# Block 0 of a WKV + FFN + routed-expert kernel: each step of a weight slice's conversion issued half a slice earlier

## The chip, the cores and the metric

The kernel runs on one core of one Trainium2 chip. The metric is device time in microseconds (us) of one execution, smaller is better. Engines are named as in the profile: PE is TensorE's matmul stream (PEld its weight loads), DVE is VectorE, ACT is ScalarE, POOL is GpSimd, SP is SyncE, which issues nearly all transfers.

## What is computed

Three layers, one after the other. The tokens are 4 sequences of 768, the model width is 8 heads of 48 (384).

```python
# 1: linear attention with a per-channel decay
for t in range(S):
    y[:, :, t] = r_t @ (state + (u * k_t) v_t^T)
    state = w * state + k_t v_t^T
# 2: gated feed-forward, d_ff = 1536
g = x @ w_gate
x = (g * sigmoid(g)) * (x @ w_val) @ w_out
# 3: one of 8 experts per token
e = argmax(x @ moe2_w_gate)
out = scale(x, e) * (relu(x @ w1[e]) @ w2[e])
```

## The kernel before

The 3072 tokens are 24 tiles of 128; three tiles form a block, so there are 8 blocks. While the feed-forward layer of block b runs, the attention of the three tiles of block b+1 is woven into it. The feed-forward width of 1536 is cut into 12 weight slices (f = 0 to 11). At the end come the experts.

**The order.** Nothing is scheduled automatically: the order in which the Python code calls the units is the order in which instructions stand in every engine's queue. `b_block` loops over the 12 slices. In iteration f it issues: the gate matmuls g(f) (`b_up`, L491), then the units in `slots[2f]`, then the down projection of slice f-2 (`b_down`, L510), then the value matmuls v(f) (L491 again), then `b_act`, then the units in `slots[2f+1]`. So a slot is half a slice, and whether a unit sits in the even or the odd slot decides whether it stands ahead of or behind `b_act` of that slice. `b_act` is four instructions: the silu on ACT (L499), **the silu product** s = silu(g) * v on DVE (L500), its rounded high part h on ACT (L502), and the remainder on POOL in block 0 (L503). In block 0 g and v use two PSUM banks in turn: g(f+1) waits for the silu of f, v(f+1) for the product of f.

**The conversion, in block 0 alone.** The weights arrive as 64-bit words. Each slice goes through these steps, in order:

- `next_w(f)` (L203): the transfer of 1152 KB by SP. From slice 4 on the data land in one of two buffers, so it waits for the conversion of slice f-2.
- `conv_low(f)` (L214): one ACT instruction takes the lowest bits out of one byte per word.
- `conv_a(f)`: six DVE instructions, three pairs of L229 (shift and or, both inputs in SBUF, result in PSUM) and L230, which make 32-bit floats, the tile `cv`.
- `conv_b(f)`: ACT rounds `cv` to the high part of W (L246), POOL subtracts for the low part (L247).
- `gate_a(f)`: three PE transposes of `cv` into PSUM bank 7 (L255) and their copy by ACT, `gt` (L257).
- `gate_b(f)`: a small product with the router's weights G (L263, bank 7 again), two small copies on ACT (L266 to `wg`, L267), one small subtraction on POOL (L268).

**Attention of a tile in block 0** (`a_place`, over 7 slots from slot 8t): scaling of krT on DVE (L332), a reduction on DVE (L350) and the diagonal matrices from it (L357, eight ACT instructions, for tiles 4 and 5; L359 on POOL for tile 3), scores into banks 6 and 7 (L379), masks on DVE (L384), output and state products (L394, L403, L440; the state product goes to bank 7), output copies (L423, L424), and the state update on DVE that reads bank 7 (`a_state_up`, L454 or L456).

Bank 7 is thus shared by the gate transposes, the gate product, half of the scores and the state product: whoever writes it next waits until the one before has been read by ACT or DVE.

Of the kernel before, what the change touches and what calls it, by code (L numbers as in the profile page):

```python
# [33 lines left out]
BT = 3  # L34
# [18 lines left out]
def kernel(  # L53
# [156 lines left out]
    def conv_low(f):  # L210
        b3 = raws[f].bitcast(U8).rearrange("p (n e) -> p n e", e=8)[:, :, 3]
        t = spare[f] if f in spare else wpool.tile([P, 2 * FG], F32, tag=f"W{f}", name=f"low{f}")
        lows[f] = t[:, 0:FW].bitcast(I32)
        act.activation(out=lows[f], in_=b3, func=AF.Identity, bias=nb, scale=1.0 / 32)  # L214

    def conv_steps(f):
        raw = raws.pop(f)
        r32 = raw.rearrange("p (n two) -> p n two", two=2)
        hi = r32[:, :, 1]
        if f % 2 == 0:  # L220
            t = cpool.tile([P, FW], I32, tag="rows", name="cv", bufs=1)
        else:
            t = apool.tile([P, FW], I32, tag="cv", name="cv", bufs=1)
        cvs[f] = t.bitcast(F32)
        n = lows.pop(f)
        p = bank[5][:, 0:DM].bitcast(I32)

        def word(o):
            dve.scalar_tensor_tensor(p, hi[:, o], 3, n[:, o], ALU.logical_shift_left, ALU.bitwise_or)  # L229
            dve.scalar_tensor_tensor(t[:, o], hi[:, o], 0x3FFFFFFF, p, ALU.bitwise_or, ALU.bitwise_and)  # L230

        return [lambda c=c: word(slice(c * DM, (c + 1) * DM)) for c in range(3)]

    def conv_a(f):
        for u in conv_steps(f):
            u()
# [3 lines left out]
    def conv_b(f, parts=(ALL,)):  # L240
        x = cvs[f]
        if f not in W:
            W[f] = wpool.tile([P, 2, FG], F32R, tag=f"W{f}", name=f"W{f}")
        for o in parts:
            hi, lo = W[f][:, 0, o], W[f][:, 1, o]
            act.copy(out=hi, in_=x[:, o])  # L246
            pool.tensor_tensor(out=lo, in0=x[:, o], in1=hi.bitcast(F32), op=ALU.subtract)  # L247
# [3 lines left out]
    def gate_a(f):  # L251
        x = cvs[f]
        for c in range(KC):
            o = (2 * KC + c) * P
            pe.transpose(bank[7][:, c * P : (c + 1) * P], x[:, o : o + P], ident)  # L255
        gts[f] = t = apool.tile([P, DM], F32, tag="gt", name="gt", bufs=1)
        act.copy(out=t, in_=bank[7][:, 0:DM])  # L257

    def gate_b(f):
        t = gts.pop(f)  # L260
        wg = bank[7][:, DM : DM + 16]
        for c in range(KC):
            pe.matmul(wg, t[:, c * P : (c + 1) * P], G[:, c, :], start=(c == 0), stop=(c == KC - 1))  # L263
        hi, lo = W[f][:, 0, FW:], W[f][:, 1, FW:]
        x = apool.tile([P, 16], F32, tag="wg", name="wg", bufs=2)
        act.copy(out=x, in_=wg)  # L266
        act.copy(out=hi, in_=x)  # L267
        pool.tensor_tensor(out=lo, in0=x, in1=hi.bitcast(F32), op=ALU.subtract)  # L268
# [176 lines left out]
    def a_state_up(i, b):  # L445
        c = i // NB
        if c == TPB - 1:
            return
        m4 = bank[b][:, 0 : 4 * HD].rearrange("s (p e) -> s p e", p=4)
        for j in range(2):  # L450
            q = slice(64 * j, 64 * j + HD)
            sv, m = Sst[i % NB][q, :, j, 0:HD], m4[q]
            if c == 0:
                dve.tensor_copy(out=sv, in_=m)  # L454
            else:
                dve.tensor_tensor(out=sv, in0=m, in1=sv, op=ALU.add)  # L456
# [6 lines left out]
    def a_out(i):  # L463
        a_out_mm(i)
        a_state_mm(i, 7)
        a_decay(i)
        a_out_ev(i)
# [142 lines left out]
    def a_place(slots, i, first):  # L610
        def load():
            if i + 1 < NT:
                a_load(i + 1)

        def load_kr():
            if i + 1 < NT:
                a_load_kr(i + 1)

        def bonus():
            if i + 1 < NT:  # L620
                a_bonus(i + 1)

        def diag():
            a_diag(i, BT < i < 2 * BT)

        def scores():
            a_scores(i)
            a_mask(i)

        slots[first].append(load)  # L630
        slots[first + (i == BT)].append(lambda: a_scale(i))
        slots[first + 1].append(diag)
        e = 1 if i % BT == BT - 1 else 0
        slots[first + 3 - e] += [lambda: a_keys(i), scores]
        slots[first + 5 - e] += [lambda: a_out(i), load_kr, bonus]
        slots[first + 6].append(lambda: a_state_up(i, 7))

    raws = {}

    def next_w(f):  # L640
        if f in (2, 3):
            raws[f] = load_w(f, spare[7 - f][:, 0 : 2 * FW].bitcast(I32))
        elif f < NF:
            raws[f] = load_w(f)
# [157 lines left out]
    with tc.manual_schedule():  # L802
# [59 lines left out]
        for blk in range(NBLK):  # L862
            slots = [[] for _ in range(2 * NF)]

            def clear(first, slot):
                slots[slot].append(lambda: [clear_slots(zts[0], i) for i in (first, first + 1)])

            if blk + 1 < NBLK:
                for t in range(BT):
                    a_place(slots, (blk + 1) * BT + t, 8 * t)  # L870
            if blk == 0:
                slots[0][0:0] = [lambda: conv_low(2), lambda: gate_b(0), lambda: conv_b(1, (GV, OUT)), lambda: gate_a(1), lambda: conv_a(2), lambda: a_state(0, 0)]
                slots[1][0:0] = [lambda: gate_b(1), lambda: conv_b(2), lambda: a_state(1, 1)]
                slots[2][0:0] = [lambda: gate_a(2), lambda: a_state(2, 2), lambda: gate_b(2)]
                for f in range(3, NF):
                    slots[2 * f - 6].append(lambda f=f: conv_low(f))
                    slots[2 * f - 5] += [lambda f=f: conv_a(f), lambda f=f: next_w(f + 2) if f > 3 else None]
                    slots[2 * f - 3].insert(0, lambda f=f: conv_b(f)); slots[2 * f - 3 + (f == 3)].insert(0, lambda f=f: gate_a(f))
                    slots[2 * f - 2].insert(0, lambda f=f: gate_b(f)) if f > 3 else slots[4].append(lambda: gate_b(3))
                slots[19].append(lambda: zts.append(late_consts()))  # L880
            else:
                for o, u in zip((4, 7, 7) if blk == NBLK - 1 else (12, 15, 15), c_units(blk - 1)):
                    slots[o].append(u)
                if blk == 1:
                    for i in range(16):
                        clear(2 * i, 2 + (2 * i) // 3)
                if 2 <= blk < 6:
                    for n in range(3):
                        for k, u in enumerate(scan_units(3 * (blk - 2) + n)):
                            slots[7 * n + 1 + 4 * k].append(u)  # L890
            if blk == NBLK - 1:
                right.close()
                rpool = right.enter_context(tc.tile_pool(name="rpool", bufs=1, side="right"))
                raws12 = [rpool.tile([P, NEF, 2 * DM], F32, name="raw12_0")]
                wfs = [rpool.tile([P, 2, 2 * DM], F32R, name=f"wf{i}") for i in range(4)]
                early = bpool.tile([P, 2, KC, BN], F32R, tag="xT", name="early", bufs=2).rearrange("s h c t -> s (h c t)")
                ge = (EARLY + P - 1) // P
                xd_e = [early[:, i * KC * EARLY : (i + 1) * KC * EARLY].rearrange("s (c t) -> s c t", c=KC) for i in range(2)]
                xs_e = cpool.tile([P, ge, RW - DM], F32, tag="xs_e", name="xs_e", bufs=1)
                xr_e = []  # L900

                def early_gather():
                    xr_e.append(cpool.tile([P, BT, DM + 16], F32, tag="rows", name="xr_e", bufs=1))
                    d_gather(xr_e[0][:, :, 0:RW], 0, EARLY)

                def early_turn(g):
                    d_turn(0, xr_e[0], xd_e, g, EARLY, 7)
                    n = min(P, EARLY - g * P)
                    pool.tensor_copy(out=xs_e[0:n, g], in_=xr_e[0][0:n, g, DM:RW])

                d_load(0)
                slots[12].append(early_gather)
                for f in range(4):
                    slots[11 + 3 * f].append(lambda f=f: d_split(f))
                for g in range(ge):
                    slots[18 + 2 * g].append(lambda g=g: early_turn(g))
            b_block(blk, slots)
# [252 lines left out]
```

## Time and profile before

| what | value |
|---|---|
| median of 3 runs | 871.21 us (870.07 to 871.34) |
| the profiled execution's own time | 870.54 us |
| its span in the trace | 868.7 us |
| PE busy | 823.9 us, 95% of the span |
| DVE, ACT, POOL busy | 55%, 33%, 32% |
| PE's share of the chain that ended last | 89% |

The profile cuts the span into 40 slices of some 21.7 us. PE's busy share is 3 tenths in the first of them, 7 or 8 tenths from the second to the sixth, and 9 tenths or more in all but two behind. Block 0 lies from 34 us (its first gate matmul) to about 139 us. The other numbers of the profile are read in the rows below. Row times are us from the start of the span, durations us, and means of one instruction ns.

### The profile page before, as it was taken

Reading aid. Unit: us, or ns where it says so; the run is one execution under the profiler, and the core shown is the slowest. Engines: PE = TensorE matmul, PEld = TensorE weight load, DVE = VectorE, ACT = ScalarE, POOL = GpSimd, SP = SyncE. Lnnn points to the kernel's source line nnn. Section 1 sums busy time; section 2 is a strip of 40 time slices with the busy share of each in tenths; the row PEclk is TensorE's granted clock in tenths of the full one; section 3 lists DMA queues with packets and bytes.
Section 4 is the critical chain, followed back from the end, with each engine's and each line's share of the span. In section 5 each row is a group of like instructions: output and inputs, shape, how many; then the busy total and the mean of one; then the engine's idle time right before and its main releaser. Section 6 shows DMA issues by size and latency. Waiting matters only on the chain.

```text
span 868.7 us, 13843 instructions
## 1 busy us (share of the span) xinstructions
PE 823.9 (95%) x5427; PEld 794.6 (91%) x5427; DVE 474.7 (55%) x923; ACT 287.2 (33%) x604; POOL 276.7 (32%) x241
## 2 busy tenths in 40 slices
PE   3878889999999999999999999999979999999996
PEld 2668789999999999999999999999979999999996
DVE  8698663354475465566565544333644655555541
ACT  2636452212212221222221222223434444444432
POOL 6766654232344335335244112010100220121022
PEclk9989999999999999999999999999989999999999
DMA  8615415833234222422323211410574443445200
GB/s 259 242 49 207 132 78 153 227 99 114 101 106 136 102 101 80 152 71 82 125 91 116 60 46 47 160 50 1 189 287 143 130 163 122 163 139 167 84 25 35
DMA packets 29768, 104.89 MB, mean 121 GB/s; under 512 B 5175, under 2 KB 14193, under 8 KB 26624
## 3 DMA queue, kind: packets, MB, share of 16 engines
q1 hardware_dynamic: 26368, 94.37, 33.6%
q0 software_dynamic: 3328, 9.56, 2.9%
q8 instruction: 45, 0.74, 0.4%
q14 instruction: 27, 0.22, 0.1%
HBM read 85.84 MB, written 16.41 MB: 118 GB/s over the span
## 4 chain that ended last, share of the span: by engine, by line
PE 89%; DVE 4%; ACT 3%; issue 2%; DMA 2%; SPq 0%; POOLq 0%; DVEq 0%; ACTq 0%
PE bank L491 34%; PE bank L510 18%; PE bank L707 12%; PE bank L724 12%; PE bank L379 3%; PE bank L403 3%; PE bank L394 2%; DVE bank L229 2%; DMA spare<-in_rkv_dram 2%; PE bank L672 1%; PE bank L738 1%; DVE cv L230 1%; PE bank L440 1%; ACT at L357 1%; ACT W L246 1%
## 5 line engine op out<-in xcount | busy, mean ns | idle before, releaser
L491 PE MATMUL bank<-xT,W 128*128 128x384 f32 x1728 | 332.7, 342 | 5.0 <-ACT s L499 4.7
L491 PEld LDWEIGHTS bank<-xT,W 128*128 128x128 f32 x1728 | 305.7, 190 | 8.5 <-ACT s L499 5.1
L510 PE MATMUL bank<-W,h 128*128 128x400 f32 x864 | 175.6, 348 | 0.0
L510 PEld LDWEIGHTS bank<-W,h 128*128 128x128 f32 x864 | 155.9, 189 | 1.7 <-issue 0.4
L502 ACT CAST h<-s 128x384 fp32r<-128x384 f32 x96 | 49.2, 513 | 309.2 <-DVE s L500 309.2
L500 DVE TENSOR_TENSOR s<-s,bank 128x384 f32<-128x384 f32 x96 | 53.0, 552 | 164.4 <-PE bank L491 138.3
L724 PE MATMUL bank<-hd,wf 128*128 128x416 f32 (+1 forms) x576 | 113.7, 343 | 0.0
L724 PEld LDWEIGHTS bank<-hd,wf 128*128 128x128 f32 x576 | 104.2, 188 | 0.6
L746 POOL DMA_INDIRECT out_dram<-yo,ix x32 | 34.4, 1074 | 207.6 <-DVE yo L742 181.6
L503 DVE TENSOR_TENSOR h<-s,h 128x384 fp32r<-128x384 f32 x84 | 60.6, 721 | 48.6 <-ACT h L502 48.6
L711 DVE SCALAR_TENSOR_TENSOR hd<-bank,hd 128x416 fp32r<-128x416 f32 (+1 forms) x64 | 36.6, 573 | 83.8 <-ACT hd L710 83.7
L359 POOL TENSOR_TENSOR at<-ident,a 128x1024 f32<-128x1024 f32 x19 | 36.4, 1914 | 136.4 <-DVE a L350 136.4
L572 POOL DMA_INDIRECT xs<-rows,slot x24 | 25.2, 1050 | 127.4 <-DVE slot L570 88.6
L656 DVE TENSOR_TENSOR wf<-raw,wf 128x768 fp32r<-128x768 f32 x64 | 61.1, 955 | 7.1 <-ACT wf L655 1.5
L707 PE MATMUL bank<-xd1h,wf 128*128 128x416 f32 x192 | 59.8, 370 | 4.6 <-issue 4.6
L499 ACT ACTIVATE s<-bank 128x384 f32<-128x384 f32 x96 | 47.1, 491 | 48.8 <-PE bank L491 48.8
L710 ACT ACTIVATE hd<-bank 128x416 fp32r<-128x416 f32 (+1 forms) x64 | 32.3, 504 | 88.8 <-PE bank L707 87.5
L655 ACT CAST wf<-raw 128x768 fp32r<-128x768 f32 x64 | 52.9, 826 | 0.0
L707 PE MATMUL bank<-xd0h,wf 128*128 128x416 f32 x144 | 43.7, 361 | 0.0
L707 PEld LDWEIGHTS bank<-xd1h,wf 128*128 128x128 f32 x192 | 37.6, 196 | 5.2 <-issue 4.8
L384 DVE COPY_PREDICATED at<-mask,bank 128x512 f32<-128x512 int32 x42 | 28.4, 727 | 16.5 <-POOL at L359 14.5
L461 POOL TENSOR_TENSOR S<-S,pw 128x512 f32<-128x512 f32 x16 | 18.0, 1127 | 58.2 <-PE bank L394 58.2
(181 smaller groups left out, 979.4 us busy)
## 6 DMA issues: line engine op xcount, KB each, us to landing
raw<-in_w_dram SPq DMA_DIRECT2D x36, 768.0 KB, 4.4
raw<-in_w_dram SPq DMA_DIRECT2D x22, 1152.0 KB, 6.9
rkv<-in_rkv_dram SPq DMA_DIRECT2D x21, 576.0 KB, 5.8
krT<-in_krT_dram SPq DMA_DIRECT2D x42, 192.0 KB, 3.4
xs<-zt SPq DMA_DIRECT2D x32, 197.0 KB, 6.4
xr<-xs SPq DMA_DIRECT2D x6, 591.0 KB, 5.7
spare<-in_w_dram SPq DMA_DIRECT2D x2, 1152.0 KB, 9.2
xT<-stage SPq DMA_DIRECT2D x42, 48.0 KB, 2.2
```

What stands on the lines that cost most here:

```text
L359: pool.tensor_tensor(out=af, in0=bc(ident, 1, [P, NH, P]), in1=bc(a, 2, [P, NH, P]), op=ALU.mult)
L491: pe.matmul(ps[i], W[f][:, wl, o : o + P], x[:, xl, c, :], start=(c == 0 and n == 0), stop=(c == KC - 1 and n == 2),)
L499: act.activation(out=s, in_=g, func=AF.Silu)
L500: dve.tensor_tensor(out=s, in0=s, in1=v, op=ALU.mult)
L502: act.copy(out=h[:, 0], in_=s)
L503: (pool if blk == 0 else dve).tensor_tensor(out=h[:, 1], in0=s, in1=h[:, 0].bitcast(F32), op=ALU.subtract)
L510: pe.matmul(bank[t][:, 0 : DM + 16], h[:, hl, t * P : (t + 1) * P], W[f][:, wl, 2 * KC * P :], start=(f == 0 and n == 0), stop=(f == NF - ...
L655: act.copy(out=wf[:, 0], in_=raw[:, f])
L656: dve.tensor_tensor(out=wf[:, 1], in0=raw[:, f], in1=wf[:, 0].bitcast(F32), op=ALU.subtract)
L707: pe.matmul(ps, wf[:, wl, c * P : (c + 1) * P], xd[xl][:, c, 0:n], start=(i == 0), stop=(i == 3 * KC - 1))
L711: dve.scalar_tensor_tensor(h[:, 1, 0:n], ps, 0.0, h[:, 0, 0:n].bitcast(F32), ALU.max, ALU.subtract)
L724: pe.matmul(bank[c][:, 0:n], wf[:, wl, o : o + P], h[:, hl, 0:n], start=(f == 0 and i == 0), stop=(f == NEF - 1 and i == 2),)
```

## The change

In block 0, for slices 3 to 11: `conv_low` moves from slot 2f-6 to slot 2f-7 (slot 0 for f = 3), `conv_a` and the transfer `next_w(f+2)` behind it from 2f-5 to 2f-6, `gate_a` and `conv_b` from 2f-3 to 2f-4 (for f = 3 `gate_a` from 4 to 3), `gate_b` from 2f-2 to 2f-3 (for f = 3 from 4 to 3). Each is half a slice earlier in all queues. `conv_a(f)` thus goes from an odd slot, behind the silu product of slice f-3, to the even slot ahead of it. The state update of the three tiles in block 0 keeps its slot (8t+6) but goes to the front of it. No instruction is added, removed or altered.

```diff
         slots[first + 5 - e] += [lambda: a_out(i), load_kr, bonus]
-        slots[first + 6].append(lambda: a_state_up(i, 7))
+        if i >= 2 * BT:
+            slots[first + 6].append(lambda: a_state_up(i, 7))
...
                 for f in range(3, NF):
-                    slots[2 * f - 6].append(lambda f=f: conv_low(f))
-                    slots[2 * f - 5] += [lambda f=f: conv_a(f), lambda f=f: next_w(f + 2) if f > 3 else None]
-                    slots[2 * f - 3].insert(0, lambda f=f: conv_b(f)); slots[2 * f - 3 + (f == 3)].insert(0, lambda f=f: gate_a(f))
-                    slots[2 * f - 2].insert(0, lambda f=f: gate_b(f)) if f > 3 else slots[4].append(lambda: gate_b(3))
+                    slots[2 * f - 4].insert(0, lambda f=f: conv_b(f))
+                    slots[2 * f - 4 + (f == 3)].insert(0, lambda f=f: gate_a(f))
+                    if f > 3:
+                        slots[2 * f - 3].insert(0, lambda f=f: gate_b(f))
+                    slots[max(0, 2 * f - 7)].append(lambda f=f: conv_low(f))
+                    slots[2 * f - 6] += [lambda f=f: conv_a(f), lambda f=f: next_w(f + 2) if f > 3 else None]
+                slots[3].append(lambda: gate_b(3))
+                for t in range(BT):
+                    slots[8 * t + 6].insert(0, lambda t=t: a_state_up(BT + t, 7))
```

What this does to the queues is shown at two places. On **DVE**, at the first slices of block 0 (`bank_66` is the scratch of the conversion; the rows with `spare_99` as first input are conv_a(3)); before:

```order
L454 COPY S_108<-bank_61 48x4x48 x2
L500 TENSOR_TENSOR s<-s,bank_65 128x384
L454 COPY S_109<-bank_62 48x4x48 x2
L332 TENSOR_TENSOR krT<-krT,WT 128x1024
L350 TENSOR_REDUCE a<-rkv 128x4x2
L229 SCALAR_TENSOR_TENSOR bank_66<-spare_99,low_405 128x384
L230 SCALAR_TENSOR_TENSOR cv<-spare_99,bank_66 128x384
```

and now:

```order
L454 COPY S_108<-bank_61 48x4x48 x2
L229 SCALAR_TENSOR_TENSOR bank_66<-spare_99,low_405 128x384
L230 SCALAR_TENSOR_TENSOR cv<-spare_99,bank_66 128x384
L229 SCALAR_TENSOR_TENSOR bank_66<-spare_99,low_405 128x384
L230 SCALAR_TENSOR_TENSOR cv<-spare_99,bank_66 128x384
L229 SCALAR_TENSOR_TENSOR bank_66<-spare_99,low_405 128x384
L230 SCALAR_TENSOR_TENSOR cv<-spare_99,bank_66 128x384
L500 TENSOR_TENSOR s<-s,bank_65 128x384
```

The first silu product (L500) stood ahead of the conversion of slice 3; now all six instructions of it stand ahead of the product. The same holds one slice later for conv_a(4) and the second product, and so on.

On **ACT**, from the silu of slice 0 to the second L502 (W_376 is slice 1; W_420 before and W_427 now are slice 2; W_455 is slice 3; `spare_99<-raw` is conv_low(4), `spare_100<-raw` is conv_low(5)); before:

```order
L499 ACTIVATE s<-bank_64 128x384
L502 CAST h<-s 128x384
L266 COPY wg<-bank_68 128x16
L267 CAST W_376<-wg 128x16
L246 CAST W_420<-cv 128x1152
L257 COPY gt<-bank_68 128x384
L266 COPY wg<-bank_68 128x16
L267 CAST W_420<-wg 128x16
L214 ACTIVATE spare_99<-raw,nb 128x1152
L499 ACTIVATE s<-bank_64 128x384
L502 CAST h<-s 128x384
```

and now:

```order
L502 CAST h<-s 128x384
L266 COPY wg<-bank_68 128x16
L267 CAST W_376<-wg 128x16
L246 CAST W_427<-cv 128x1152
L214 ACTIVATE spare_99<-raw,nb 128x1152
L246 CAST W_455<-cv 128x1152
L257 COPY gt<-bank_68 128x384
L266 COPY wg<-bank_68 128x16
L267 CAST W_427<-wg 128x16
L499 ACTIVATE s<-bank_64 128x384
L502 CAST h<-s 128x384
L257 COPY gt<-bank_68 128x384
```

Two long instructions, L214 of slice 4 and L246 of slice 3, came in ahead of the gate copy L257 of slice 2, and the gate copy of slice 3 now stands behind the second L502.

## Rows read from the trace of the kernel before

**Rows 1.** Busy time by stretch in block 0 (view by windows: length, then each engine's busy time, TensorE clock, DMA).

```profile
34.00:56.30 22.30, 14.38 (x124) 12.38 (x124) 19.91 (x30) 11.38 (x20) 16.25 (x12) 0.92 0.49 186
56.30:74.70 18.40, 15.53 (x107) 14.27 (x108) 14.22 (x22) 8.67 (x17) 12.36 (x9) 0.91 0.26 87
74.70:91.30 16.60, 14.16 (x91) 12.68 (x89) 13.67 (x18) 12.16 (x25) 9.76 (x8) 0.99 0.61 223
91.30:114.80 23.50, 21.58 (x150) 20.77 (x149) 18.82 (x27) 10.69 (x20) 15.83 (x12) 0.94 0.47 161
114.80:137.80 23.00, 20.46 (x146) 19.53 (x145) 10.46 (x17) 9.33 (x24) 14.03 (x16) 0.93 0.05 10
```

**Rows 2.** Who waited for whom, TensorE from 137.8 us to the end.

```profile
PE bank L707 <- issue: 4.6, 1, 4.6
```

**Rows 3.** Timeline of VectorE (start, length, engine, line, operation; in brackets the idle time before).

```profile
43.51 0.66 DVE L229 SCALAR_TENSOR_TENSOR bank<-spare,low 128x384 int32<-128x384 int32 x1
...
45.43 0.55 DVE L500 TENSOR_TENSOR s<-s,bank 128x384 f32<-128x384 f32 x1
...
49.07 2.74 DVE L229 SCALAR_TENSOR_TENSOR bank<-spare,low 128x384 int32<-128x384 int32 x1
...
91.02 1.34 DVE L384 COPY_PREDICATED at<-mask,bank 128x512 f32<-128x512 int32 x2 [1.96 <-PE bank L379]
```

**Rows 4.** Timeline of ScalarE, the same columns.

```profile
46.01 0.51 ACT L502 CAST h<-s 128x384 fp32r<-128x384 f32 x1 [3.15 <-DVE s L500]
46.43 0.17 ACT L266 COPY wg<-bank 128x16 f32<-128x16 f32 x1
...
46.74 1.15 ACT L246 CAST W<-cv 128x1152 fp32r<-128x1152 f32 x1
...
54.59 1.33 ACT L214 ACTIVATE spare<-raw,nb 128x1152 int32<-128x1152 uint8 x1 [4.93 <-DVE cv L230]
...
84.11 2.46 ACT L357 ACTIVATE at<-ident,a 128x128 f32<-128x128 f32 x8
```

**Rows 5.** Timeline of TensorE, the same columns.

```profile
46.65 0.55 PE L255 MATMUL bank<-ident,cv 128*128 128x128 f32 x3 [0.61 <-ACT wg L266]
...
48.32 0.84 PE L263 MATMUL bank<-G,gt 128*128 128x16 f32 x6 [0.63 <-ACT gt L257]
49.01 1.82 PE L491 MATMUL bank<-xT,W 128*128 128x384 f32 x9
...
56.35 2.95 PE L491 MATMUL bank<-xT,W 128*128 128x384 f32 x9 [4.43 <-ACT s L499]
...
74.45 0.52 PE L255 MATMUL bank<-ident,cv 128*128 128x128 f32 x3 [1.85 <-DVE S L454]
74.72 1.82 PE L491 MATMUL bank<-xT,W 128*128 128x384 f32 x9
...
90.03 1.34 PE L379 MATMUL bank<-krT 64*128 64x128 f32 x14 [0.94 <-ACT gt L257]
91.31 3.18 PE L491 MATMUL bank<-xT,W 128*128 128x384 f32 x9
...
114.80 1.81 PE L491 MATMUL bank<-xT,W 128*128 128x384 f32 x9
...
126.62 1.82 PE L491 MATMUL bank<-xT,W 128*128 128x384 f32 x9
```

**Rows 6.** Groups by line and shape from 34 to 138 us (count, busy time, mean ns of one).

```profile
L229 DVE SCALAR_TENSOR_TENSOR bank<-raw,spare 128x384 int32<-128x384 int32 x24 | 27.7, 1153 | 0.6
L247 POOL TENSOR_TENSOR W<-cv,W 128x1152 fp32r<-128x1152 f32 x10 | 26.8, 2684 | 2.8 <-ACT W L246 2.8
...
L230 DVE SCALAR_TENSOR_TENSOR cv<-raw,bank 128x384 int32<-128x384 int32 x27 | 14.9, 554 | 1.3
```

**Rows 7.** DMA issues of SyncE over the kernel (count, size, median us to landing).

```profile
raw<-in_w_dram SPq DMA_DIRECT2D x22, 1152.0 KB, 6.9
rkv<-in_rkv_dram SPq DMA_DIRECT2D x21, 576.0 KB, 5.8
```

## The prediction

> **What bounds the kernel now.** I read the busy shares of the page first (table above), then block 0 by windows, then who waits, then the timelines of its engines. From 137.8 us on TensorE waits for another engine nowhere in the trace; its one wait is 4.6 us of issue [rows 2]. So whatever block 0 gains or loses reaches the end unchanged, and only block 0 has slack. There PE is busy 86.1 of the 103.8 us from 34.0 to 137.8 [rows 1]: 17.7 us are idle, 7.9 of them ahead of 56.3. [...] The wait that the change is aimed at is seen at 74.45: gate transposes wait 1.85 us for the state copy (L454) on VectorE, which stood behind a conversion [rows 5].
>
> **What one conversion costs.** Undisturbed, an L229 takes about 0.6 us (0.66 in [rows 3]) and an L230 0.55 [rows 6]; three pairs with 0.03 us between instructions are 3.5 us. In the mean of block 0 an L229 takes 1.15 us [rows 6], so the mean conversion is 3 x (1.15 + 0.55) + 0.2 = 5.3 us. The long L229s (2.74 us at 49.07 [rows 3]) lie beside POOL's subtractions of 2.68 us [rows 6]. The longest that I allow is three L229s that each wait for one POOL instruction, about 7 us.
>
> [...]
>
> **The start of block 0, step by step.** No instruction is added or removed; all of the cost is in the order.
> - DVE: conv_a(3) comes ahead of the product of slice 0 (45.43 [rows 3]), in a stretch where its L229 are short. The product goes to 45.43 + 3.5 = 48.9.
> - ACT: the rounding L502 (46.01) and, behind it, the copy L266 of slice 1's gate (46.43) wait for that product and move by the same 3.5 [rows 4].
> - PE: the transposes of gate_a(2) need bank 7 and so that copy: from 46.65 [rows 5] to 50.1. PE has nothing else in its queue meanwhile.
> - ACT: between L246 of slice 2 and the gate copy there now stand L214 of slice 4 (1.33) and L246 of slice 3 (1.15) [rows 4], 2.3 us with their overlap at the edges. PE's gate_b(2) goes from 48.32 [rows 5] to 48.32 + 3.5 + 2.3 = 54.1, and v(1) from 49.01 to 54.8.
> - DVE: conv_a(4) now stands ahead of the product of slice 1. It starts when L214(4) is done and POOL's L247 of slice 2 lets it, at about 54.6, and ends between 54.6 + 5.3 = 59.9 and 54.6 + 7 = 61.6; since three POOL instructions stand beside it, I take 60.9. The product follows (0.55), then L502 (0.51), then the gate copy of slice 3 (some 0.5): 62.4. Fourteen of the sixteen score matmuls (1.34 [rows 5]) wait for that copy in bank 7, the masks L384 (1.34 [rows 3]) wait for the scores, gate_b(3) (0.84) for the masks, and g(2) stands behind it: 62.4 + 1.34 + 1.34 + 0.84 = 65.9. It was 56.35: **+9.6 us**.
>
> **Regained.** From there to g(4) at 74.72 the kernel needed 18.4 us, of which PE idled 2.9 [rows 1] and lost some 1.2 to the low clock in g(2) (2.95 against 1.82) [rows 5]. With the state update at the head of its slot and conv_a(5) done while PE has work, I leave 0.4 of this: 18.4 - 3.7 = 14.7, g(4) at about 80.6. That is -3.7; **+5.9** remains.
>
> **The new loop.** Before, ACT takes the low bits of slice f+4 (L214, behind L502 of slice f) while DVE still converts slice f+3. Now conv_a(f+4) is the next conversion behind product f, and its L214 still stands behind L502 of slice f, which waits for that product. So the chain product 0.55, L502 0.51, two gate copies 0.4, L214 1.33, conversion 5.3 is serial: 8.1 us a slice, and DVE idles for 2.2 of it. Where a tile's output copies stand between, I add 1.5, an estimate between nothing and some five instructions of 0.5.
> - v(2) ends some 5.7 us behind the start of g(2) (three groups of nine matmuls and three transposes [rows 5], less their overlap), and product 2 starts at 71.6. Product 3: + 8.1 + 1.5 = 81.2. Product 4: 89.3. Ahead of product 5 stands also tile 4's reduction (0.5) and its diagonal on ACT (2.46 [rows 4]): + 8.1 + 3.0 = 100.4. Then L502 and a gate copy (0.7) and the 14 scores (1.34): g(6) at 102.4, against 91.31 [rows 5]: **+11**.
> - From g(6) to g(9) it was 23.5 us (91.31 to 114.80), of which 1.9 idle [rows 1]. Now product 6 is bound by PE, at about 108.6; product 7, with the outputs of tile 4, at 118.2; g(9) stands about 6 us behind that: 124.2, **+9.4**.
> - g(9) to g(10) was 11.8 us [rows 5]. Now tile 5's diagonal (2.46), the gate copy behind it, the scores, a down projection and v(9) hang behind product 8, at 126.3: 11 us more give g(10) at 137.3, against 126.62: **+10.7**. With the longest conversion in place of the mean at one of these places it is up to +12.4. I take the middle, +11.5.
> - Behind slice 11 nothing is left to convert and PE is bound by itself in both orders.
>
> The profiled execution took 870.54 us, 0.67 below the median of 871.21. With +11.5 it would be 882.0; against the median, **882.7**.
>
> **Queues that cost nothing.** SyncE now issues slice 7's load ahead of tile 4's krT. Slice 6's buffer comes free at 60 to 61, its L214 comes at about 74: 13 us for a landing of 6.9 [rows 7]. The rkv load of tile 5 goes out behind slice 8's at about 81 and is first read by the reduction near 89: 8 us against 5.8 [rows 7]; if this cover is gone, each us more is a us in the diagonal of product 5. POOL's subtractions move ahead of the remainders of h (L503), which the down projection needs only two slices later.
>
> **Rivals.**
> 1. *It does what it was moved for* (faster). The product waited for PE several times, so an earlier conversion fills DVE's idle time, and gate transposes and state copies never hold PE. This decides if conversions end ahead of v(f). In the stretches behind 56.3 the idle time of PE is 2.9 + 2.4 + 1.9 + 2.5 = 9.8 us [rows 1]; all of it gone gives 861, half 866. Against it: DVE ends conv_a(3) at 48.9 where v(0) was long done, and conv_a(4) some 3 us behind v(1). Chance 0.05.
> 2. *Start lost, then regained* (no difference). The +9.6 comes, and the 9.8 us of idle time behind it go: 871. It needs the loop of 8.1 us to be hidden by PE's slice, 86.1 / 12 = 7.2 us with the tiles' work [rows 1], so it needs conversions near 3.5 us in place of 5.3. Chance 0.05.
> 3. *The start alone* (slower). If L214 is done early and the scores of tiles 4 and 5 wait no longer than before, +5.9 stays: 877. Chance 0.15.
> 4. *Worse*: PE's longer idle times cost more half-clock groups. One such group costs 1.1 to 1.4 us (2.95 or 3.18 against 1.82 [rows 5]); three more (4 us) and a longer conversion in one place (1.7) give +17, 888. Chance 0.07.
>
> [...]
>
> **How the numbers follow.** The forecast has 0.68, its own range being +8.5 to +15 by the conversion's 3.5 to 7 us in two places and one slow group either way. Its neighbours 3 and 4 go the same way: slower by over 0.2% (1.7 us, about what a measurement of this kernel can tell from no change) 0.90, within it 0.05, faster 0.05. For 8 in 10 I take 876 (rival 3 and a little) to 888 (rival 4).
>
> **What would show it.** In the profile after: the first L500 near 49; L255 of gate_a(2) idle some 4 us or more behind ACT's wg copy; g(2) near 66, g(6) near 102, g(10) near 138; L229 waiting for ACT's L214 by 1 to 2 us in most slices; PE idle in block 0 of 25 us or more in place of 17.7; no wait of PE behind 150 us. I am wrong if g(2) comes before 60, or if L500 waits for PE in most slices.

## The result and the profile after

The changed kernel takes **878.43 us** (median of 5 runs, 876.53 to 878.91), the kernel before in the same rounds 871.21 us (869.94 to 872.88). The ratio is 1.0081, 95% interval 1.0063 to 1.0099: slower by 0.8%. The forecast was 882.7 us with a range of 876 to 888. The profiled execution took 878.91 us, its span is 877.2 us, 8.5 us above the 868.7 us of before.

Block 0 first, by windows whose edges are the same events as in [rows 1] (the start, g(2), g(4), g(6), g(9) and v(11)), so that the lengths can be subtracted row by row. Columns: length, busy time of PE, PEld, DVE, ACT, POOL, TensorE clock, DMA.

```profile
35.00:66.90 31.90, 19.60 (x133) 17.01 (x132) 27.10 (x42) 14.14 (x24) 19.30 (x15) 0.74 0.42 164
66.90:82.30 15.40, 15.15 (x106) 14.59 (x105) 7.79 (x14) 7.00 (x14) 7.95 (x7) 0.87 0.33 104
82.30:105.30 23.00, 14.76 (x90) 13.47 (x90) 15.11 (x20) 12.07 (x26) 11.11 (x10) 0.92 0.42 152
105.30:128.30 23.00, 21.68 (x149) 20.67 (x148) 15.86 (x26) 10.50 (x19) 12.47 (x11) 0.93 0.36 123
128.30:152.50 24.20, 20.74 (x140) 19.38 (x140) 7.55 (x12) 7.86 (x22) 12.71 (x16) 0.86 0.05 10
```

Against [rows 1] the five stretches are +9.6, -3.0, +6.4, -0.5 and +1.2 us: **+13.7 us** in block 0. PE is busy 91.9 us in them (86.1 before) and idle 25.6 (17.7 before). Another 1.0 us comes from ahead of the change: the run as a whole reaches block 0 later (the first L184 of DVE at 40.96, before 39.95). So v(10), at 133.04 before, is at 147.73: +14.7. (Over the twelve profiles of this case that first L184 lies between 38.3 and 43.4 us, so the 1.0 us is not put down to the change.) Yet the span grew by 8.5 only. The rest of this section follows both numbers.

**The start of block 0.** The timeline of TensorE (start, length, line, operation; in brackets the idle time before and what ended it):

```profile
51.05 0.90 PE L255 MATMUL bank<-ident,cv 128*128 128x128 f32 x3 [3.88 <-ACT wg L266]
...
55.01 1.46 PE L263 MATMUL bank<-G,gt 128*128 128x16 f32 x6 [2.25 <-ACT gt L257]
56.31 3.23 PE L491 MATMUL bank<-xT,W 128*128 128x384 f32 x9
...
63.27 1.32 PE L379 MATMUL bank<-krT 64*128 64x128 f32 x14 [2.40 <-ACT gt L257]
65.71 1.47 PE L263 MATMUL bank<-G,gt 128*128 128x16 f32 x6 [1.12 <-DVE at L384]
67.02 3.23 PE L491 MATMUL bank<-xT,W 128*128 128x384 f32 x9
```

These are gate_a(2), gate_b(2), v(1), the scores of tile 3, gate_b(3) and g(2), the groups of [rows 5]. g(2) was at 56.35. Each of the four waits has ACT or DVE behind it, and the first is led back by their timelines to the silu product. DVE in the same stretch:

```profile
49.83 0.55 DVE L500 TENSOR_TENSOR s<-s,bank 128x384 f32<-128x384 f32 x1
...
54.22 1.94 DVE L229 SCALAR_TENSOR_TENSOR bank<-raw,spare 128x384 int32<-128x384 int32 x1
56.27 0.55 DVE L230 SCALAR_TENSOR_TENSOR cv<-raw,bank 128x384 int32<-128x384 int32 x1
56.86 1.48 DVE L229 SCALAR_TENSOR_TENSOR bank<-raw,spare 128x384 int32<-128x384 int32 x1
58.37 0.55 DVE L230 SCALAR_TENSOR_TENSOR cv<-raw,bank 128x384 int32<-128x384 int32 x1
58.96 2.29 DVE L229 SCALAR_TENSOR_TENSOR bank<-raw,spare 128x384 int32<-128x384 int32 x1
61.28 0.55 DVE L230 SCALAR_TENSOR_TENSOR cv<-raw,bank 128x384 int32<-128x384 int32 x1
61.75 0.55 DVE L500 TENSOR_TENSOR s<-s,bank 128x384 f32<-128x384 f32 x1
```

Product 0 is at 49.83 (45.43 in [rows 3]), because conv_a(3) stands ahead of it. The six rows from 54.22 are conv_a(4), 7.6 us with three long L229s; product 1 stands behind it. POOL in the same stretch:

```profile
53.12 2.62 POOL L247 TENSOR_TENSOR W<-cv,W 128x1152 fp32r<-128x1152 f32 x1
55.70 2.21 POOL L359 TENSOR_TENSOR at<-ident,a 128x1024 f32<-128x1024 f32 x1
57.87 2.95 POOL L247 TENSOR_TENSOR W<-cv,W 128x1152 fp32r<-128x1152 f32 x1
```

These three end at 55.74, 57.91 and 60.82, and the three L229s end 0.42 to 0.43 us behind them, at 56.16, 58.34 and 61.25: so each lasts until a POOL instruction is done. And ACT:

```profile
50.41 0.51 ACT L502 CAST h<-s 128x384 fp32r<-128x384 f32 x1 [6.54 <-DVE s L500]
50.83 0.16 ACT L266 COPY wg<-bank 128x16 f32<-128x16 f32 x1
...
51.13 1.15 ACT L246 CAST W<-cv 128x1152 fp32r<-128x1152 f32 x1
52.19 1.35 ACT L214 ACTIVATE spare<-raw,nb 128x1152 int32<-128x1152 uint8 x1
53.44 1.15 ACT L246 CAST W<-cv 128x1152 fp32r<-128x1152 f32 x1
54.48 0.48 ACT L257 COPY gt<-bank 128x384 f32<-128x384 f32 x1
```

The copy of the gate (L257) follows three long instructions where one stood before, and PE's gate_b(2) at 55.01 starts behind it.

**The loop behind it.** DVE again, the waits of conversions for the low bits that ACT takes (L214), and the product behind the second of them:

```profile
86.70 0.57 DVE L229 SCALAR_TENSOR_TENSOR bank<-raw,spare 128x384 int32<-128x384 int32 x1 [1.02 <-ACT spare L214]
...
91.97 0.55 DVE L500 TENSOR_TENSOR s<-s,bank 128x384 f32<-128x384 f32 x1
...
96.97 0.57 DVE L229 SCALAR_TENSOR_TENSOR bank<-raw,spare 128x384 int32<-128x384 int32 x1 [3.99 <-ACT spare L214]
...
102.19 0.55 DVE L500 TENSOR_TENSOR s<-s,bank 128x384 f32<-128x384 f32 x1
```

The products 2 to 5 start at 74.30, 84.00, 91.97 and 102.19: 9.7, 8.0 and 10.2 us apart. For none of the last three did DVE wait for PE. In the conversions ahead of these three the third L229 is long (2.40, 2.32 and 2.27 us, against 0.57 for the second), and it ends 0.42 to 0.43 us behind the end of POOL's subtraction of the slice before (83.07, 91.04, 101.26): some 1.8 us of each step. The 3.99 us of idle time are ACT's, where the diagonal matrices of tile 4 stand between the gate copy and the low bits:

```profile
93.28 2.45 ACT L357 ACTIVATE at<-ident,a 128x128 f32<-128x128 f32 x8
95.63 1.31 ACT L214 ACTIVATE spare<-raw,nb 128x1152 int32<-128x1152 uint8 x1
```

On PE this ends in the waits of gate transposes and scores; the largest of PE from 34 to 148 us (us in total, times, longest):

```profile
PE bank L255 <- ACT wg L266: 9.9, 5, 3.9
PE bank L379 <- ACT wg L266: 4.8, 1, 4.8
PE bank L379 <- ACT gt L257: 3.9, 2, 2.4
PE bank L263 <- ACT gt L257: 2.7, 2, 2.2
```

The 4.8 us are the scores of tile 4, ahead of g(6), which starts at 105.41 (91.31 in [rows 5]).

**The place where 6 us came back.** Silu by silu the shift stays at 14.7 us through all the blocks behind block 0 and the first expert. It falls in one place, at PE's branch on the flag of the routing (`if` with the label "size", which picks the capacity of the experts that follow), at 632.6 us before and 647.3 us after. The kernel before, TensorE (L724 is the last group ahead of the branch, L707 the first behind it):

```profile
632.57 1.44 PE L724 MATMUL bank<-hd,wf 128*128 128x288 f32 x9
638.60 0.71 PE L707 MATMUL bank<-xd1h,wf 128*128 128x416 f32 x1 [4.59 <-issue]
639.10 0.55 PE L707 MATMUL bank<-xd1l,wf 128*128 128x416 f32 x1
```

That is the wait of [rows 2]. The same place after the change (one line lower in the file):

```profile
647.27 1.45 PE L725 MATMUL bank<-hd,wf 128*128 128x288 f32 x9
648.55 0.34 PE L708 MATMUL bank<-xd1h,wf 128*128 128x416 f32 x1
648.81 0.46 PE L708 MATMUL bank<-xd1l,wf 128*128 128x416 f32 x1
```

The wait is gone, and so are the first matmuls at the low clock behind it (granted clock 0.59 of full from 638.6 to 645.0 before, 1.00 from 648.5 to 655.0 after). The trace's record of the branch instruction itself is 5.88 us before and 0.39 us after; with the slow matmuls the shift falls by 6.9 us to 7.8. The change does not touch the experts. 1.0 + 13.7 - 6.9 is 7.8 of the 8.5 us of the spans; 0.7 lie in small pieces behind the branch.

### The profile page after: what moved, and what is told of

Same layout as the page of the kernel before. It is cut to its first block, busy times and chain, and to the rows that moved or that the text cites. A ratio compares the mean times of both kernels' runs of the same rounds, so it can differ in the third digit from the quotient of the medians.

```text
span 877.2 us, 13838 instructions
## 1 busy us (share of the span) xinstructions
PE 828.2 (94%) x5427; PEld 797.9 (91%) x5427; DVE 472.3 (54%) x923; ACT 287.0 (33%) x604; POOL 274.3 (31%) x241
## 4 chain that ended last, share of the span: by engine, by line
PE 87%; DVE 6%; ACT 2%; issue 2%; DMA 1%; POOL 1%; SPq 0%; POOLq 0%; DVEq 0%; ACTq 0%
PE bank L491 33%; PE bank L510 17%; PE bank L708 12%; PE bank L725 12%; DVE bank L229 3%; PE bank L403 3%; PE bank L379 3%; PE bank L394 2%; DVE cv L230 1%; PE bank L673 1%; PE bank L739 1%; DMA spare<-in_rkv_dram 1%; ACT spare L214 1%; PE bank L440 1%; ACT at L357 1%
## 5 line engine op out<-in xcount | busy, mean ns | idle before, releaser
L502 ACT CAST h<-s 128x384 fp32r<-128x384 f32 x96 | 49.2, 513 | 324.9 <-DVE s L500 324.9
L500 DVE TENSOR_TENSOR s<-s,bank 128x384 f32<-128x384 f32 x96 | 52.9, 551 | 168.6 <-PE bank L491 143.1
L708 PE MATMUL bank<-xd1h,wf 128*128 128x416 f32 x192 | 58.0, 359 | 0.0
L247 POOL TENSOR_TENSOR W<-cv,W 128x1152 fp32r<-128x1152 f32 (+2 forms) x14 | 33.6, 2405 | 24.6 <-ACT W L246 24.6
L379 PEld LDWEIGHTS bank<-krT 64*128 64x128 f32 x336 | 23.4, 200 | 14.6 <-issue 5.2
```

The source lines that it names most:

```text
L379: pe.matmul(bank[b0 + j][:, p * P : (p + 1) * P], k, r, start=True, stop=True)
L500: dve.tensor_tensor(out=s, in0=s, in1=v, op=ALU.mult)
L502: act.copy(out=h[:, 0], in_=s)
L708: pe.matmul(ps, wf[:, wl, c * P : (c + 1) * P], xd[xl][:, c, 0:n], start=(i == 0), stop=(i == 3 * KC - 1))
```

## The experiments

The question was first what had removed the wait at the branch, and then which part of the change makes the 13.7 us. For each run two numbers are read from its trace beside the time: the length of block 0 from the first L184 of DVE to v(10), which leaves out what happens ahead of the change (93.1 us before, 106.8 after), and the record of the branch.

### 1. Two tiny matmuls more in the changed kernel

The change adds and removes nothing in the program's code, yet it had left PE four instructions fewer ahead of the branch: the trace shows 80 semaphore instructions there before and 76 after, and the same number of weight loads and matmuls. This run puts four back (each tiny matmul is a weight load and a matmul), far from block 0, ahead of everything else that PE does.

```diff
+        for _ in range(2):
+            pe.matmul(bank[7][:, 0:1], triu, ones[:, 0:1], start=True, stop=True)
```

> The changed kernel with two tiny extra matmuls (four PE instructions) ahead of everything PE does, so that PE's instruction count ahead of the 'size' branch is that of the kernel before again. Theory A (place of the branch in PE's instruction stream): PE's compare-and-branch takes some 5.9 us again, the first expert matmul behind it waits 4 to 5 us for 'issue', and the time is 878.4 + 7 = 885 us. Theory B (the stall of before came from what else was going on at that moment, the change only shifted it): nothing changes, 878 us, branch 0.4 us. Block 0 as in the changed kernel in both: v(10) starts at 147.7 us in the trace.

885.37 us (883.03 to 886.86), ratio to the kernel before 1.0154 (1.0125 to 1.0183). Block 0 is 106.2 us, as in the changed kernel. The branch took 5.92 us, and the wait stands there again:

```profile
651.32 0.71 PE L708 MATMUL bank<-xd1h,wf 128*128 128x416 f32 x1 [4.63 <-issue]
```

So the wait belongs to the place of the branch in PE's instruction stream and not to anything that block 0 does in time. With it the change costs 14 us.

### 2. and 3. The same in the kernel before: 252 instructions, and 16

The kernel before with 126 (and 8) of these matmuls at the same place.

> [...] Theory B: 871 to 875 us, the branch still takes 5.9 us. Block 0 as before: v(10) near 133 us plus what the start loses.

> The kernel before with 8 tiny matmuls (16 PE instructions) early. [...] With four fewer the stall was gone and with as many it was there, so a step of 16 upward finds it there if the edge lies just below (871, the likelier), and gone if the bad places are few.

With 252: 865.25 us (863.12 to 866.54; if the place of the branch decides, 871.2 - 7 = 864 was expected), ratio 0.9923 (0.9896 to 0.9950); the branch took 0.39 us, block 0 is unchanged at 93.2 us. It beats both kernels though it does more work. With 16: 865.58 us (864.89 to 866.96), ratio 0.9928 (0.9910 to 0.9947); block 0 is 93.2 us, but the branch took 1.99 us, a value between 5.9 and 0.4 us, of which I had expected the one or the other. PE's waits from 150 us on are then two small ones, and of another kind:

```profile
PE bank L707 <- ACT ys L731: 0.7, 1, 0.7
PE bank L718 <- ACT hf L701: 0.2, 1, 0.2
```

Behind the 0.7 us the matmuls are fast, the first in 0.45 us where it is 0.71 in the kernel before.

So the price is not simply high or low. Counted against the kernel before, it is 5.9 us at the same count (experiment 1) and at two instructions less (experiments 7, 8 and 9), 0.4 us at three less (experiment 4) and four less (the changed kernel, experiments 5 and 6), 2.0 us at 16 more and 0.4 us at 252 more (experiments 2 and 10).

The same branch is dear or cheap by where it lies among the instructions, and with 252 more it is as cheap as with four less (0.39 us both). What PE waits for there is not shown by the traces; 5.9, 2.0 and 0.39 us are what the runs show.

### 4. The start left as it was: slices 3 and 4 in their old slots

```diff
-                for f in range(3, NF):
+                for f in range(5, NF):
...
+                for f in (3, 4):
+                    slots[2 * f - 6].append(lambda f=f: conv_low(f))
+                    slots[2 * f - 5] += [lambda f=f: conv_a(f), ...]
```

> The changed kernel with slices 3 and 4 in the slots of the kernel before, slices 5 to 11 moved. Theory 1: g(2) starts at 56 to 57 us as before (the first 9.7 us come from slices 3 and 4 alone), but the loop and the scores of tile 4 cost most of it again: v(10) near 144 us, against 133.0 before and 147.7 after. Rival (the start alone is the loss): v(10) near 135 us or earlier, as the later slices then only gain.

872.88 us (870.96 to 875.39), ratio 1.0014 (0.9999 to 1.0030), a time not told apart from that of the kernel before, with the branch at 0.39 us. g(2) is at 56.20, where it was before, but block 0 is 102.3 us, **+9.2**. The start is repaired and the loop behind it costs by itself. (Slices 3 and 4 were put back with all their units; that it is conv_a ahead of the product that makes the start late is read from the timelines above.) Against the changed kernel only 4.5 us are saved, not the 9.6 that the start had lost. The wait of tile 4's scores is as in the changed kernel:

```profile
97.50 2.07 PE L379 MATMUL bank<-krT 64*128 64x128 f32 x14 [4.80 <-ACT wg L266]
```

### 5. and 6. The low bits another half slice earlier

If the loop product, rounding, gate copies, low bits, conversion is what binds, L214 ahead of the silu of its slice breaks it. Once for all slices, once for slices 6 to 11 alone:

```diff
-                    slots[max(0, 2 * f - 7)].append(lambda f=f: conv_low(f))
+                    slots[max(0, 2 * f - 8)].append(lambda f=f: conv_low(f))
```

```diff
-                    slots[max(0, 2 * f - 7)].append(lambda f=f: conv_low(f))
+                    slots[max(0, 2 * f - 7 - (f > 5))].append(lambda f=f: conv_low(f))
```

> The changed kernel with conv_low one more half slice ahead, so that L214 of slice f+4 stands ahead of the silu and of L502 of slice f on ACT. Theory 1 (the loop product, L502, gate copies, L214, conversion, product is serial and sets the slices behind the start): the waits of L229 for L214 (6.7 us in all) go, DVE starts each conversion at once, v(10) comes 3 to 4 us earlier than 147.7, and the time behind equal branches falls by as much. Rival (DVE is bound by the conversions themselves, or PE by the start alone): v(10) moves by less than 1 us. If the weight load is not there yet, L214 holds up the silu: up to 2 us worse.

> The changed kernel with conv_low half a slice earlier for slices 6 to 11 alone, so that the start is that of the changed kernel. Theory 1 (serial loop through ACT's L214): from g(2) to v(10), which took 80.7 us in the changed kernel, it takes 77 us; the waits of L229 for L214 (6.7 us there) fall under 2 us; the branch keeps its 0.4 us and the time falls from 878.4 to 874 to 875 us. Rival (it only shifts the wait to the silu, which then stands behind L214 and its load): 80 to 81 us, time within 1 us of 878.4.

All slices: 875.85 us (874.72 to 877.81), ratio 1.0038 (1.0023 to 1.0052), block 0 105.0 us, 1.8 us less where 3 to 4 were expected. At the start it costs, since ACT then takes the low bits of slice 4 ahead of the first silu, and g(1) waits for that:

```profile
49.97 3.15 PE L491 MATMUL bank<-xT,W 128*128 128x384 f32 x9 [6.77 <-ACT s L499]
```

From slice 6 on: 874.41 us (874.04 to 876.58), ratio 1.0029 (1.0016 to 1.0041), block 0 104.0 us. From g(2) to v(10) it is 77.2 us in place of 80.7, and behind g(2) no conversion waits for L214 any more. The loop is real, and its waits for the low bits are worth 3.5 us. They are not the whole of it: the conversion itself, with the L229 that waits for POOL (2.27 to 2.40 us in the changed kernel, the others 0.57), still stands between two products. What that part is worth no run shows by itself.

### 7. The diagonal matrices of tiles 4 and 5 on POOL

```diff
-            a_diag(i, BT < i < 2 * BT)
+            a_diag(i, False)
```

> The changed kernel with the diagonals of tiles 4 and 5 made by POOL (one instruction of some 1.9 us) in place of ACT (eight, 2.45 us). Theory 1 (the stalls of PE ahead of the scores of tiles 4 and 5 are the chain reduction, diagonal on ACT, L214 or gate copy, conversion, product, gate copy): g(6) comes 1 to 2.5 us earlier, g(10) 4 us earlier in all, v(10) at 143 to 144 us against 147.7. Rival (POOL is as late, its diagonal and the L229 exclude each other): no gain, or a loss of up to 2 us.

881.45 us (878.55 to 883.97), ratio 1.0114 (1.0091 to 1.0137). The time says worse, the profile says why: the branch is at 5.89 us (two instructions more on PE), and block 0 is 102.9 us, 3.9 below the changed kernel. At tile 4 the expected gain did not come: g(6) is 0.5 us later than in the changed kernel, not 1 to 2.5 us earlier. The gain lies at tile 5: from g(9) to g(10) 9.9 us in place of 13.6. The scores there wait 0.15 us (1.49 in the changed kernel), and they and the down projection behind them are fast:

```profile
130.47 1.16 PE L379 MATMUL bank<-krT 64*128 64x128 f32 x14 [0.15 <-ACT gt L257]
131.56 1.90 PE L510 MATMUL bank<-W,h 128*128 128x400 f32 x9
```

The changed kernel takes 2.07 and 2.86 us for these two.

### 8. Slices 3 and 4 alone, in the kernel before

```diff
+                for f in (3, 4):
+                    slots[2 * f - 4].insert(0, lambda f=f: conv_b(f))
...
+                    slots[2 * f - 6] += [lambda f=f: conv_a(f), ...]
...
-                for f in range(3, NF):
+                for f in range(5, NF):
```

> The kernel before with slices 3 and 4 alone moved as in the change, slices 5 to 11 in their old slots. Theory 1: g(2) starts 9.7 us later than before, near 66, and half of it is regained while DVE and PE find their old rhythm: v(10) 4 to 6 us later than before. With the run that leaves slices 3 and 4 in their old slots (+9.2 us from the same point of the start) the two make the 13.7 us of the whole change. Rival (the parts don't add, the later slices lose only since the start does): v(10) as late as with the whole change, +13 us.

878.31 us (877.08 to 880.55), ratio 1.0073 (1.0048 to 1.0099), with a branch of 5.97 us. g(2) is at 65.75 and block 0 100.8 us: **+7.7**. That is more than the 4 to 6 us expected: two slices of nine give over half of the loss.

### 9. The state update alone, in the kernel before

```diff
+        if i >= 2 * BT:
+            slots[first + 6].append(lambda: a_state_up(i, 7))
...
+                for t in range(BT):
+                    slots[8 * t + 6].insert(0, lambda t=t: a_state_up(BT + t, 7))
```

> The kernel before with the state update alone at the front of its slot; every conversion step stays where it was. Theory A: in the old order of the conversion the early state update hurts by itself. The gate product of that slot then waits in bank 7 for the state copy, which stands behind conv_a on DVE, so block 0 grows by 6 to 10 us at v(10) (counted from the first L184, before 93.1), and the whole by as much: 877 to 881 us, ratio 1.007 to 1.012. Theory B: the state update was only in the way (the wait of 1.85 us at 74.45 in the kernel before), and alone it gains: v(10) 91 to 93, ratio 0.997 to 1.000. No instruction is added, so both expect a branch on the size as in the kernel with slices 3 and 4 alone moved or in the kernel before, near 5.9 us. The loss of slices 3 and 4 alone (+7.7) and of all the rest (+9.2) add up to 16.9, and the change's is 13.7: if A holds, a part of the +9.2 is this unit's.

887.05 us (884.91 to 891.76), ratio 1.0183 (1.0141 to 1.0226), branch 5.94 us, block 0 110.9 us: **+17.8**, more than the whole change and more than theory A had allowed. PE's two largest waits from 34 to 160 us are new:

```profile
PE bank L263 <- DVE S L454: 5.5, 1, 5.5
PE bank L263 <- DVE S L456: 5.3, 1, 5.3
```

In the old order gate_b of that slot stands behind the state copy in the program and needs the same bank 7, and the state copy stands behind a conversion on DVE. So each of these two waits has the length of a conversion (72.20 to 76.88 on DVE) and the copy, with a slow down projection behind it (3.35 us both times, 1.87 at 78.51 in the changed kernel). With the gate a half slice earlier this does not happen: in the changed kernel the transposes wait 0.25 us for the state copy, where they waited 1.85 [rows 5]. Slices 3 and 4 alone cost +7.7, all but these +9.2, and the state update, which is in the second of these, +17.8 alone, against +13.7 for the whole: parts of such a reordering don't add up. No run has the change without the state update, so what it is worth beside the others is not shown but for the waits of 0.25 and 1.85 us.

### 10. The kernel before with both gains

The diagonals of tiles 4 and 5 on POOL, and 125 tiny matmuls (250 instructions) at the start.

```diff
-            a_diag(i, BT < i < 2 * BT)
+            a_diag(i, False)
...
+        for _ in range(125):
+            pe.matmul(bank[7][:, 0:1], triu, ones[:, 0:1], start=True, stop=True)
```

> The kernel before with the diagonal matrices of tiles 4 and 5 made on POOL in place of ACT, and 250 PE instructions of tiny products at the start so that the branch on the size stands in a cheap place. A (the diagonals on ACT hold up the copies of the gate in the kernel before too): v(10) counted from the first L184 0.5 to 2 us below 93.1, branch 0.39 us, time 863 to 865 us, ratio 0.990 to 0.993. B (in the old order they are hidden, POOL's extra work costs DVE as much): v(10) 93 to 94.5, 865 to 867 us, ratio 0.993 to 0.996, no better than the 865.25 us of the padding alone.

**861.49 us** (859.73 to 862.93), ratio 0.9879 (0.9859 to 0.9899), the fastest of all; branch 0.39 us, block 0 89.1 us, 4 us below the kernel before and more than theory A gave. The wait of tile 5's scores for ACT's gate copy is gone, and the down projection behind them takes 1.88 us in place of 3.31 (at a granted clock of 0.51, from 121.50 to 124.60). Before:

```profile
120.41 1.16 PE L379 MATMUL bank<-krT 64*128 64x128 f32 x14 [2.20 <-ACT wg L266]
121.50 3.31 PE L510 MATMUL bank<-W,h 128*128 128x400 f32 x9
```

and here:

```profile
119.19 1.54 PE L379 MATMUL bank<-krT 64*128 64x128 f32 x16
120.67 1.88 PE L510 MATMUL bank<-W,h 128*128 128x400 f32 x9
```

The interval touches that of the padding alone (0.9896 to 0.9950), which ran in another set of rounds, so that the diagonals' share of the time, about 4 us, is known no better than that.

### All together

| kernel | block 0, us | branch, us | sum, us | median, us |
|---|---|---|---|---|
| before, 252 more | 93.2 | 0.39 | 865.3 | 865.25 |
| before | 93.1 | 5.88 | 871.1 | 871.21 |
| before, 16 more | 93.2 | 1.99 | 865.3 | 865.58 |
| changed | 106.8 | 0.39 | 878.9 | 878.43 |
| changed, 4 more (1) | 106.2 | 5.92 | 884.2 | 885.37 |
| start as before (4) | 102.3 | 0.39 | 874.4 | 872.88 |
| low bits earlier, all (5) | 105.0 | 0.39 | 877.1 | 875.85 |
| low bits from slice 6 (6) | 104.0 | 0.39 | 876.1 | 874.41 |
| diagonals on POOL (7) | 102.9 | 5.89 | 880.9 | 881.45 |
| slices 3 and 4 alone (8) | 100.8 | 5.97 | 878.8 | 878.31 |
| state update alone (9) | 110.9 | 5.94 | 888.9 | 887.05 |
| before, diagonals and 250 (10) | 89.1 | 0.39 | 861.2 | 861.49 |

The sum is 865.25 us, plus block 0 less 93.2, plus 6.0 (871.21 less 865.25) where the branch took 5.9 us; the branch of 1.99 us is taken as free. It meets every median within 2 us, though each length of block 0 is that of one profile and the medians come from several sets of rounds. Two places thus account for the twelve kernels. The rest of the traces bears it out: from v(10) to the end of the span the six kernels with a branch of 0.39 us take 728.6 to 729.5 us, the one with 1.99 us 730.0, and the five with 5.9 us 735.5 to 736.6.

## Why the prediction was right, and where it was not

**Right in direction, place and mechanism.** The five stretches were forecast as +9.6, -3.7, +5.1, -1.6 and +2.1 (with the middle of +10.7 and +12.4 at the end); they are +9.6, -3.0, +6.4, -0.5 and +1.2.

- *The start.* Product 0 forecast at 48.9, with the 1.0 us of the late start 49.9: it is at 49.83. gate_b(2) 55.1, it is 55.01. g(2) 66.9, it is 67.02. conv_a(4), for which I took 6.3 us between 5.3 and 7, measured 7.6, beyond the upper end, but it started earlier (54.22, forecast 55.6) and so ended at 61.83 (61.9). That g(2) is met within 0.1 us is thus in part luck: two errors of some 1.3 us cancel.

  The L229s are 1.94, 1.48 and 2.29 us here, beside POOL's subtractions and diagonal, and 0.57 us at other places (86.70, 96.97). The 6.3 us let the conversion start when POOL's first subtraction was done; it started 1.5 us ahead of that one's end (55.74) and waited.
- *The loop.* Three steps forecast at 9.6, 8.1 and 11.1 us measured 9.7, 8.0 and 10.2. The L229s wait for L214, 6.7 us in five places, and experiment 6 took 3.5 us out by moving L214. The sign "by 1 to 2 us in most slices" was not met: the five waits are 0.3, 1.0, 4.0, 0.3 and 1.0 us.
- *SyncE's covers held.* In block 0 no engine waits for a transfer (before, ACT did twice, 2.4 us in all).
- *Idle time of PE.* 25 us or more forecast, 25.6 measured.

**Undersized:** the term +11.5 is 13.7. The start came out as forecast; the 2.2 us lie behind it (0.7, 1.3 and 1.1 too little in the three stretches from g(2) to g(9), 0.9 too much in the last). One part is work at the low clock that was counted at the full one: v(2) was to end 5.7 us behind the start of g(2) and ends 7.2 us behind it, since g(2) is at the low clock as before (3.23 us, granted clock 0.50 from 67.02 to 70.10; 2.95 us, 0.57 from 56.35 to 59.20 before), the transposes behind it take 0.84 and the down projection 2.07; and the scores of tile 4 at 103.41 took 2.07 (granted clock 0.50), not 1.34 (0.83 from 90.03 to 91.30 before). Another is a slip in the sum: between the start of product 5 and the scores of tile 4 it has L502 and a gate copy, but not the product's own 0.55 us. A third is a wait of ACT for the outputs of tile 4 on PE, 1.1 us ahead of its copy at 114.82, in the step to product 7. PE's busy time in the five stretches grew by 5.8 us with the same 618 matmuls, but 5.2 of it lies in the first stretch (v(1) 1.4, the gate products at 55.01 and 65.71 with 1.46 and 1.47 where 0.84 stood in [rows 5]), whose length was met.

**The step that failed** is "whatever block 0 gains or loses reaches the end unchanged". I had the row in hand, PE's wait of 4.6 us on "issue" [rows 2], and took it for a fixed cost since the change adds and removes no work there. But which instructions wait on semaphores changes with the order, PE's program became four semaphore instructions shorter ahead of the branch, and the branch fell from 5.88 to 0.39 us (experiment 1 puts it back, 2 and 3 take most or all of the 5.5 us from the kernel before). 13.7 in place of 11.5 and 6.9 given back in place of nothing: the forecast of 882.7 is 4.3 us too high, and without the branch it would have been 2 to 3 us too low (experiment 1, with the branch dear again, has 885.37). The time lies within the stated range with the branch dear or cheap. That it is not at the lower end of the range is luck: with the 11.5 us of the forecast and the cheap branch it would have been about 876 us.

**The rivals.** *It does what it was moved for* fell at the first product. *Start lost, then regained* fell: behind g(4) the loss grows again by 7.1 us (6.4, -0.5 and 1.2), and experiment 4 shows that the steps behind the start lose 9.2 us by themselves. *The start alone* (877) is near the measured time, but for the wrong reason: the block did not stop at +5.9. *Worse* (888) was right in part. v(1) is one more slow group of nine (3.23 us at a granted clock of 0.50; 1.82 at 1.00 in [rows 5]), not three: from 34 to 160 us the changed kernel has five such groups above 2.5 us, the kernel before four.

Not every stall of PE brings a slow group. Behind the waits of 3.88 and 2.25 us, of 1.12 and of 4.79 us one follows (v(1), g(2) and g(6), 3.23 us each at a granted clock of 0.50); behind the wait of 1.98 us of the transposes at 93.19 the next groups run at the full clock (1.87 us, 1.00 from 93.49 to 95.20). A price for each stall is too much: experiment 1 has seven slow groups, three more than the kernel before, and its block 0 is no longer for it (106.2 us, 106.8 in the changed kernel).

## What to carry to other kernels

Before an instruction is issued earlier, look at what it then stands ahead of in each queue: a conversion of 5 us ahead of a product of 0.55 us puts its whole length into every chain that goes through the product. Test the parts of a reordering alone and together, since a part may cost more alone than the whole does.

And compare two orders of a kernel only after looking at what the trace calls issue: here a branch far behind the change moved the result by 6 to 7 us because the program was four instructions shorter. A row that shows waiting for nothing is no fixed cost (4.6 us before, none after).

## What the hardware showed that was not expected

One branch of PE cost 5.9, 2.0 or 0.39 us by the count of instructions ahead of it, with an edge between two and three instructions less than in the kernel before (read across kernels of different order). Padding of 252 instructions saved 6 to 7 us (ratio 0.9923), more than any change of order tried here. Why 16 instructions give a value in between, and where further edges lie, was not tried and stays open.
